# A linear-attention chunk: seven masked products per pair of heads, or one with keys and receptances scaled about the chunk's middle

## The chip, the core and the metric

The kernel runs on one core of a Trainium2 chip. Times are microseconds on the device from the first to the last instruction. A core has five instruction streams that run side by side and wait for each other by semaphores: TensorE (PE: matrix products; its weight loads are shown as PEld), VectorE (DVE), ScalarE (ACT), GpSimd (POOL), and SyncE (SP), which here only starts DMA transfers. An engine with a q behind its name (SPq, ACTq, POOLq) is its sequencer, as when it starts a DMA.

## The reference

Two blocks follow each other. The first is a recurrence over 768 steps for 4 batches of 8 heads with 48 channels:

```python
for t in range(S):
    cur = einsum('bhd,bhe->bhde', u[None] * kt, vt)
    y[:, :, t] = einsum('bhd,bhde->bhe', rt, state + cur)
    state = w[None, :, :, None] * state + einsum('bhd,bhe->bhde', kt, vt)
```

`w`, the decay of each channel, is drawn as `np.random.rand(n_heads, head_dim) * 0.1 + 0.85`, so it lies in 0.85 to 0.95. The 3072 rows of y (4 x 768 tokens, 8 x 48 = 384 columns) go into the second block: gate logits `x @ w_gate` for 8 experts, a greedy balanced assignment (each expert takes exactly 384 tokens, in the order of the logits), and for each expert `relu(x @ w1) @ w2` with a hidden width of 1024. All of it is float32.

## The kernel before

Four stages follow each other on one core.

The **attention stage** (`attention`, L25 to L268) cuts the 768 steps into six chunks of 128. A unit is one chunk of one batch, all 8 heads; there are 24 units, the four batches of a chunk one after the other, so a unit's state comes from four units earlier. Steps stand on the 128 partitions. Two heads are handled together (a pair, four pairs), each padded from 48 to 64 channels.

For a unit, `scale` (L138) loads k, r and v, turns k and r with PE transposes (L146, L151), copies them out of PSUM on ACT (L148, L153), and makes for each of seven levels (64, 32, .., 1 steps) a scaled copy of the keys (POOL, L160) and of the receptances (DVE, two per level for the two heads of a pair, L167; on ACT at the last level, L169). `pairs` (L193) makes for each level four products of 128 x 128 (L200) and lets DVE write those (s, t) that belong to the level into AT, the matrix of pair weights, by a masked copy (L204). `outputs` (L208) multiplies the receptances with the state (L218) and AT with v (L225), adds each step's own term (L228) into x, and brings the state forward (L233, L237, L241). `gate` (L245) turns a unit's x (L251), copies it out on ACT (L253), and multiplies it with the gate's weights (L256) into the logits LG (L258). The written order is `scale(n+1)`, `pairs(n)`, `gate(n-1)`, `outputs(n)`; a scheduler may move instructions of neighbouring units past each other on an engine.

At the end of the stage, x of all tokens and LG lie in SBUF. The **assignment stage** (`assignment`, L271) finds the experts by seven rounds on LG, with small products and DVE operations that wait for each other. Then the rows of x are **scattered** to DRAM in the experts' order (L531), and the **experts stage** (L555 to L576) reads them back and does the two products (L563, L570). The weights of the first two experts are loaded during the attention stage (`before_unit`, L518; L513 and L515): SP starts them as soon as their place in SP's queue is reached.

Of the kernel before, what the change touches and what calls it, by code (L numbers as in the profile page):

```python
# [10 lines left out]
F32 = mybir.dt.float32  # L11
BF16 = mybir.dt.bfloat16
I32 = mybir.dt.int32
U8 = mybir.dt.uint8
AF = mybir.ActivationFunctionType
ALU = mybir.AluOpType
AX = mybir.AxisListType
PSUM = bass.MemoryType.PSUM

NEG = -3.4028234663852886e38  # L20
T = 128
PD = 64


def attention(ctx, tc, r, k, v, w, u, wg, x_all, LG, ident, before_unit):  # L25
    """The recurrence in chunks of 128 steps, and the gate's logits.

    Within a chunk, the pairs (s, t) with s < t are split by halving: at level
    h (64, 32, .., 1) a block of 2h steps has its middle m between s and t, and
    w^(t-1-s) = w^(m-1-s) * w^(t-m), powers from 0 to h-1 only, so that no  # L30
    value of w needs a negative power.
    """
    nc = tc.nc
    B, H, S, D = r.shape
    DX = H * D
    C = S // T
    HP = H // 2
    E = wg.shape[1]
    LEVELS = [64, 32, 16, 8, 4, 2, 1]

    const = ctx.enter_context(tc.tile_pool(name="a_const", bufs=1))
# [26 lines left out]

    # powers of w, with the channels on the partitions: (head of the pair, d)
    wpow = const.tile([128, 8, HP], F32, name="wpow")  # L70
# [29 lines left out]

    # the pairs (s, t) of each level, t over the upper halves
    mask_f = const.tile([128, len(LEVELS), PD], F32, name="mask_f")
# [9 lines left out]

    # The keys of a level count in its lower halves only. The receptances of a
    # pair of heads stand in blocks, so that one product serves both heads.
    ATs, Ks, Rs = [], [], []
# [20 lines left out]
    live = {}  # L136

    def scale(n):  # L138
        """Transposed keys and receptances, and each level's copies of them."""
        load(n + 2)  # L140
# [29 lines left out]

        # a step's own term: r . (u * k) for each head
        rk = pool.tile([128, DX], F32, name="rk")
# [9 lines left out]

        # what reads and writes the state
        rw = kw = None
# [8 lines left out]
    def pairs(n):  # L193
        """The sums over the channels for the pairs of steps of a chunk."""
        kT, K, R, AT = (live[n][x] for x in ("kT", "K", "R", "AT"))
# [12 lines left out]
    def outputs(n):  # L208
        """x, and the state behind the chunk."""
        b, c = units[n]  # L210
# [58 lines left out]


def assignment(ctx, tc, ML, dest, CAP):  # L271
    """Each token's row in the order of the experts.

    The greedy walk down the sorted logits, from one filled expert to the next:
    while no further expert fills, each token goes to its best open one, so the
    next to fill is the one whose CAP-th best token comes first, at the largest
    value that has CAP tokens at or above it for some expert. That value is found
    by its bits, four at a time. Equal logits go by expert and by token.
    """
    nc = tc.nc  # L280
# [32 lines left out]
    for g in range(8):  # L313
        nc.vector.tensor_single_scalar(out=steps[:, g, :], in_=digits, scalar=28 - 4 * g,
                                       op=ALU.logical_shift_left)
    # floats in their order: key = bits ^ (sign ? ~0 : 1 << 31)
    top = const.tile([128, ND], I32, name="top")
# [21 lines left out]
    for _ in range(E - 1):  # L339
        # each token's best open expert  # L340
        m = pool.tile([128, NT], F32, name="m")
# [8 lines left out]

        # the value at which the next expert fills
        cand, bits = top, None
# [28 lines left out]

        # the expert that fills there
        ge = pool.tile([128, NT], F32, name="ge")
# [19 lines left out]

        # its tokens: those above the value, and the first of those at it
        pf = pool.tile([128, NT, E], F32, name="pf")
# [26 lines left out]

        # they and their expert leave
        nc.vector.scalar_tensor_tensor(out=eid, in0=acc, scalar=estar, in1=eid, op0=ALU.mult, op1=ALU.add)
# [5 lines left out]

    # the rest are the last expert's
    rest = pool.tile([128, NT], F32, name="rest")
# [28 lines left out]
def rwkv5_eagle_then_base_layer_balanced(  # L471
# [27 lines left out]
    make_identity(nc, ident)  # L499
    # the rows of x, each with its token's number behind it  # L500
    x_all = keep.tile([128, NT, DX + 1], F32, name="x_all")
# [5 lines left out]
    weights = {}  # L507

    def load_weights(e):
        if e >= E:  # L510
            return
        w1 = wpool.tile([128, KD, F], F32, name="w1")
        nc.sync.dma_start(w1, moe_w1[e].rearrange("(c p) f -> p c f", p=128))  # L513
        w2 = wpool.tile([128, KF, DX], F32, name="w2")
        nc.sync.dma_start(w2, moe_w2[e].rearrange("(c p) d -> p c d", p=128))  # L515
        weights[e] = (w1, w2)

    def before_unit(n):  # L518
        if n in (8, 14):
            load_weights((n - 8) // 6)  # L520

    with ExitStack() as part:
        attention(part, tc, r, k, v, w, u, moe_w_gate, x_all, LG, ident, before_unit)
    with ExitStack() as part:
        assignment(part, tc, LG, dest, CAP)

    # every token has a row of its own, in the experts' order as in out
    xs_rows = dram_disjoint_views(xs_dram, NT)
# [76 lines left out]
```

## Time and profile before

| what | value |
|---|---|
| time, median of 3 runs | 865.85 us (864.2 to 866.3) |
| profiled execution, its span from first to last instruction (the page gives no other time for it) | 865.4 us |
| PE busy | 615.8 us (71%) |
| DVE busy | 457.5 us (53%) |
| POOL busy | 293.0 us (34%) |
| ACT busy | 92.4 us (11%) |

The shares are means over four stages that have little in common. The page cuts the span into 40 slices of 21.6 us; in its lines of busy tenths and of the granted PE clock they stand apart:

```profile
PE   2478899998999988832223322202999999999996
DVE  5968988999989988656665566601001001001000
POOL 7976677686776734000000000073011001001001
PEclk9989999999999999855555555555999999999999
```

A digit is the busy share of a slice in tenths; PEclk is the clock granted to TensorE in tenths of full speed, where 9 or more is its level of 2.4 GHz and 5 its level of 1.2 GHz. The first 17 slices are the attention stage, with PE, DVE and POOL all busy; then comes the assignment with DVE at two thirds and PE at half its clock, then the scatter on POOL, then the experts with PE alone.

### The profile page before, as it was taken

The page shows a single profiled execution, that of the slowest core. Times are in us where ns is not written, and L with a number is a line of the kernel's source. Part 1 is how long each engine was busy: PE and PEld are TensorE (multiplying, and loading weights), DVE is VectorE, ACT ScalarE, POOL GpSimd, SP SyncE. Part 2 cuts the span into 40 slices and gives each one's busy share as a digit, 9 for nine tenths or more (in the row PEclk, how much of TensorE's full clock was granted, in tenths as well). Part 3 has the DMA queues.
Part 4 walks back from the last instruction along what each step waited for, and adds up shares of the span by engine and source line. Part 5 has one row for each costly group of instructions (what it writes and reads, how often), then busy time and mean ns, then how long its engine had stood idle before and what let it go on. Part 6 is the DMA issues. An engine that isn't in the chain of part 4 may idle for free.

```text
span 865.4 us, 11948 instructions
## 1 busy us (share of the span) xinstructions
PE 615.8 (71%) x4723; PEld 486.1 (56%) x4723; DVE 457.5 (53%) x1143; ACT 92.4 (11%) x210; POOL 293.0 (34%) x395
## 2 busy tenths in 40 slices
PE   2478899998999988832223322202999999999996
PEld 1477888888888887722222212101556656656653
DVE  5968988999989988656665566601001001001000
ACT  1011111211112111000000000000110110110110
POOL 7976677686776734000000000073011001001001
PEclk9989999999999999855555555555999999999999
DMA  9252212222122200000000000034334434424100
GB/s 244 94 132 42 47 38 47 47 47 47 37 47 47 47 11 1 1 1 2 1 1 1 1 2 1 1 137 151 114 100 132 170 101 147 163 92 138 45 18 27
DMA packets 93687, 54.48 MB, mean 63 GB/s; under 512 B 76864, under 2 KB 88256, under 8 KB 93632
## 3 DMA queue, kind: packets, MB, share of 16 engines
q1 hardware_dynamic: 86400, 39.33, 16.8%
q0 software_dynamic: 3072, 9.45, 2.9%
q10 hardware_dynamic: 4160, 4.94, 1.7%
q8 instruction: 37, 0.61, 0.3%
q14 instruction: 18, 0.15, 0.1%
HBM read 44.26 MB, written 9.45 MB: 62 GB/s over the span
## 4 chain that ended last, share of the span: by engine, by line
PE 38%; issue 29%; DVE 26%; DMA 2%; POOL 2%; SPq 1%; ACT 0%; POOLq 0%; DVEq 0%; ACTq 0%
DVE AT L204 15%; PE h_ps L563 14%; PE o_ps L570 14%; DVE R L167 8%; PE y_ps L225 6%; PE g_ps L200 2%; DMA w<-in_moe_w_dram 2%; DVE x_all L228 1%; SPq L66 1%; DVE state L241 1%; PE xT_ps L551 1%; POOL K L160 1%; DVE dd L177 1%; DMA xg<-x_sorted 0%; POOL rk L175 0%
## 5 line engine op out<-in xcount | busy, mean ns | idle before, releaser
L200 PE MATMUL g_ps<-R,K 128*128 128x128 f32 x1152 | 152.2, 285 | 4.9 <-DVE AT L204 4.0
L204 DVE COPY_PREDICATED AT<-mask,g_ps 128x512 f32<-128x512 uint8 x168 | 147.8, 882 | 9.3 <-PE g_ps L200 2.3
L200 PEld LDWEIGHTS g_ps<-R,K 128*128 128x128 f32 x1152 | 142.9, 200 | 7.9 <-issue 6.3
L570 PE MATMUL o_ps<-w,hid 128*128 128x384 f32 x384 | 126.2, 486 | 0.0
L563 PE MATMUL h_ps<-xT,w 128*128 128x384 f32 x384 | 125.7, 487 | 0.0
L167 DVE TENSOR_TENSOR R<-rT_ps,pw 64x256 f32<-64x256 f32 x288 | 121.9, 423 | 5.3 <-ACT rT L153 1.5
L160 POOL TENSOR_TENSOR K<-kT,rv 128x256 f32<-128x256 f32 x144 | 94.9, 694 | 84.7 <-ACT kT L148 84.7
L359 PE MATMUL cnt<-prop,ind 128*15 128x8 bf16 x1344 | 42.1, 166 | 97.2 <-DVE ind L337 62.9
L359 PEld LDWEIGHTS <-ind 128*15 128x15 bf16 x1344 | 37.1, 90 | 115.8 <-DVE ind L337 105.9
L563 PEld LDWEIGHTS h_ps<-xT,w 128*128 128x128 f32 x384 | 73.1, 191 | 51.2 <-DVE xT L552 0.4
L570 PEld LDWEIGHTS o_ps<-w,hid 128*128 128x128 f32 x384 | 71.9, 190 | 47.4
L531 POOL DMA_INDIRECT x_sorted<-x_all,dest x24 | 23.3, 970 | 203.7 <-DVE dest L467 196.7
L573 POOL DMA_INDIRECT out_dram<-o_sb,tok x24 | 23.2, 968 | 200.6 <-DVE o_sb L572 175.7
L552 DVE COPY xT<-xT_ps 128x384 f32<-128x384 f32 x24 | 12.7, 555 | 147.8 <-PE xT_ps L551 147.7
L564 ACT ACTIVATE hid<-h_ps 128x384 f32<-128x384 f32 x64 | 31.5, 492 | 445.9 <-PE h_ps L563 445.9
L572 DVE COPY o_sb<-o_ps 128x384 f32<-128x384 f32 x24 | 13.4, 558 | 121.9 <-PE o_ps L570 121.9
L225 PE MATMUL y_ps<-vt,AT 128*128 128x48 f32 x384 | 49.3, 283 | 11.1 <-DVE AT L204 11.0
L225 PEld LDWEIGHTS y_ps<-vt,AT 128*128 128x128 f32 x384 | 46.3, 197 | 15.6 <-DVE AT L204 15.6
L551 PE MATMUL xT_ps<-ident,xg 128*128 128x128 f32 x72 | 11.7, 298 | 40.6 <-DMA xg<-x_sorted 40.5
L151 PE MATMUL rT_ps<-ident,rpad 128*128 128x128 f32 x96 | 23.6, 301 | 16.4 <-ACT R L169 15.7
L551 PEld LDWEIGHTS xT_ps<-ident,xg 128*128 128x128 f32 x72 | 9.6, 154 | 45.5 <-issue 42.2
L361 DVE TENSOR_SCALAR full<-cnt 15x8 bf16<-15x8 f32 x56 | 8.6, 153 | 47.3 <-PE cnt L359 47.3
(133 smaller groups left out, 652.4 us busy)
## 6 DMA issues: line engine op xcount, KB each, us to landing
w<-in_moe_w_dram SPq DMA_DIRECT2D x16, 1536.0 KB, 7.2
xg<-x_sorted ACTq DMA_DIRECT2D x8, 577.5 KB, 6.3
kpad<-in_k_dram SPq DMA_DIRECT2D x24, 192.0 KB, 2.6
rpad<-in_r_dram SPq DMA_DIRECT2D x24, 192.0 KB, 2.6
vt<-in_v_dram SPq DMA_DIRECT2D x24, 192.0 KB, 2.7
x_sorted<-x_all,dest POOLq DMA_INDIRECT x24
out_dram<-o_sb,tok POOLq DMA_INDIRECT x24
u_bc<-in_u_dram ACTq DMA_DIRECT2D x1, 192.0 KB, 4.2
```

The source lines that it names most:

```text
L151: nc.tensor.transpose(rT_ps[:, a, :], pair(rt, a), ident)
L160: nc.gpsimd.tensor_mul(half(K[h], h, 0), half(kT, h, 0), by)
L167: nc.vector.tensor_mul(dst, src, by)
L200: nc.tensor.matmul(g_ps[:, a].rearrange("p q i -> p (q i)"), keys[:, a, :], R[h][:, a].rearrange("p q i -> p (q i)"), start=True, stop=True)
L204: nc.vector.copy_predicated(out=half(AT, h, 1), mask=mk.unsqueeze(1).to_broadcast([128, H, nb, h]), data=g_ps.rearrange("p a q (n i) -> p ...
L225: nc.tensor.matmul(y_ps[:, ds(h * D, D)], AT[:, h, :], vt[:, ds(h * D, D)], start=first, stop=(h == H - 1), skip_group_check=True)
L359: nc.tensor.matmul(cnt, ind[:, i, :], prop[:, i, :], start=(i == 0), stop=(i == NT - 1))
L531: nc.gpsimd.indirect_dma_start(out=xs_rows[i], out_offset=bass.IndirectOffsetOnAxis(ap=dest[:, i:i + 1], axis=0), in_=x_all[:, i, :], in_o ...
L551: nc.tensor.transpose(xT_ps[:, f, :], xg[:, c, ts(f, 128)], ident)
L563: nc.tensor.matmul(h_ps, w1[:, f, ts(j, 128)], xT[:, f, :], start=(f == 0), stop=(f == KD - 1))
L564: nc.scalar.activation(hid[:, j, :], h_ps, AF.Relu)
L570: nc.tensor.matmul(o_ps, hid[:, j, ts(c, 128)], w2[:, j, :], start=(j == 0), stop=(j == KF - 1))
```

## The change

Before the attention stage, DVE tests whether all 384 values of w lie in 0.7 to 1.2. Each engine reads the answer into a register and branches. In that range, `attention_mild` runs; otherwise `attention_any`, which is the old `attention` with nothing in it changed. Both stand in the program.

`attention_mild` writes w^(t-1-s) as w^(t-65) * w^(64-s): the keys of step s are multiplied with w^(64-s), the receptances of step t with w^(t-65). Positive and negative powers both occur (exponents up to 65). These scales are made once (wk, wr, steps on partitions, by powers and reciprocals, L355 and L357), so that a unit scales k and r with one DVE product each before they are turned. One product of 128 x 256 per pair of heads then gives all pairs (s, t) of both heads; DVE multiplies it with a triangle mask into AT. The scaled keys and receptances serve the state as well. Heads are not padded: a pair stands on 96 partitions. ACT writes each head's receptances into a block of its own by a scale of 1 or 0 per partition. The written order runs one step further ahead: `scale(n+2)`, `turn(n+1)`, `pairs(n)`, `outputs(n-1)`, `gate(n-2)`. The core of the diff:

```diff
+def decays_are_mild(ctx, tc, w):
+    nc.sync.dma_start(row, w.rearrange("h d -> (h d)").unsqueeze(0))
+    nc.vector.tensor_single_scalar(out=ge, in_=row, scalar=W_MIN, op=ALU.is_ge)
+    nc.vector.scalar_tensor_tensor(out=both, in0=row, scalar=W_MAX, in1=ge, op0=ALU.is_le, op1=ALU.mult)
+    nc.vector.tensor_reduce(out=flag, in_=both, axis=AX.X, op=ALU.min)
+    return nc.values_load(flag[0:1, 0:1])
...
+    for j in range(7):                      # in attention_mild: powers of w
...
+        nc.vector.tensor_mul(up[:, :, n:n + m], up[:, :, 0:m], by)
+        nc.gpsimd.tensor_mul(down[:, :, L + 1 - n - m:L + 1 - n], down[:, :, L + 1 - m:L + 1], by)
+        nc.vector.tensor_mul(wp[:, j + 1, :], wp[:, j, :], wp[:, j, :])
...
+            nc.vector.reciprocal(ch[:, :, M + 1:T], up[:, :, 1:T - M])
...
+    def scale(n):
...
+        nc.vector.tensor_mul(ks, kt, wk)
+        nc.vector.tensor_mul(rs, rt, wr)
+        nc.gpsimd.tensor_mul(rk, rt, kt)
+        nc.gpsimd.tensor_mul(rk, rk, u_bc)
+        nc.vector.tensor_reduce(out=dd, in_=rk.rearrange("p (h d) -> p h d", h=H), axis=AX.X, op=ALU.add)
+        nc.gpsimd.tensor_mul(yd.rearrange("p (h d) -> p h d", h=H), ...)
+    def turn(n):
...
+        nc.scalar.copy(kT, kT_ps)
+        for q in range(2):
+            nc.scalar.activation(rB[:, :, q, :], rT_ps, AF.Copy, scale=own[:, q:q + 1])
...
+            nc.scalar.copy(rT, rT_ps)
+    def pairs(n):
+        for a in range(HP):
+            nc.tensor.matmul(g_ps[:, 2 * a:2 * a + 2, :].rearrange("p q t -> p (q t)"), kT[:, a, :],
+                             rB[:, a].rearrange("p q t -> p (q t)"), start=True, stop=True)
+        for z in range(2):
+            nc.vector.tensor_mul(AT[:, hs, :], g_ps[:, hs, :], mask.unsqueeze(1).to_broadcast([128, HP, T]))
...
+    for n in range(N + 1):
+        if n + 2 < N:
+            scale(n + 2)
+        if n + 1 < N:
+            turn(n + 1)
+        if n < N:
+            pairs(n)
+        if n > 0:
+            outputs(n - 1)
+        if n > 1:
+            gate(n - 2)
...
     with ExitStack() as part:
-        attention(part, tc, r, k, v, w, u, moe_w_gate, x_all, LG, ident, before_unit)
+        mild = decays_are_mild(part, tc, w)
+    with ExitStack() as part:
+        with tc.If(mild > 0) as which:
+                attention_mild(arm, *arguments)
+        with which.Else():
+                attention_any(arm, *arguments)
```

In `attention_mild` every PSUM tile has one buffer, against two or four for some before. `outputs` and `gate` issue the same products as before (L446, L450, L458, L473, L478), with the state added as a whole on DVE (L462) and multiplied with the chunk's decay on POOL (L463).

On **PE in the steady part of the attention stage**, the rows of one unit before: kT_ps and rT_ps are the turned keys and receptances, g_ps the pair products of a level, y_ps the outputs, kv_ps the new state, xT_ps and lg_ps the gate.

```order
L251 MATMUL xT_ps<-ident,x_all 128x128 x3
L218 MATMUL y_ps<-state_225,rw 128x96 x4
L256 MATMUL lg_ps<-wg_sb,xT 128x8 x3
L233 MATMUL kv_ps<-vt,kw 128x96 x4
L146 MATMUL kT_ps<-ident,kpad_88 128x128 x4
L151 MATMUL rT_ps<-ident,rpad_91 128x128
L200 MATMUL g_ps<-R_1_206,K_1_200 128x128 x4
L200 MATMUL g_ps<-R_1_207,K_1_201 128x128 x4
L151 MATMUL rT_ps<-ident,rpad_91 128x128
L200 MATMUL g_ps<-R_1_208,kT 128x128 x4
L151 MATMUL rT_ps<-ident,rpad_91 128x128 x2
```

The same engine in the same part with the change, one whole unit (ks and rs are the scaled keys and receptances, rB the blocks):

```order
L473 MATMUL xT_ps<-ident,x_all 128x128 x3
L411 MATMUL rT_ps<-ident,rs 96x128 x3
L408 MATMUL kT_ps<-ident,ks 96x128 x2
L478 MATMUL lg_ps<-wg_sb,xT 128x8 x3
L408 MATMUL kT_ps<-ident,ks 96x128 x2
L411 MATMUL rT_ps<-ident,rs 96x128
L428 MATMUL g_ps<-rB,kT 128x256 x4
L446 MATMUL y_ps<-state_190,rT 128x96 x4
L450 MATMUL y_ps<-vt,AT 128x48 x8
L458 MATMUL kv_ps<-vt,ks 96x96 x4
```

Seven groups of four g products became one with twice the columns; between kv_ps of a unit and the next turned keys stand six transposes, three of the gate and three of the receptances. A product of this list stands in the trace as two instructions where its operands are multiplied in float32, and as one where it is a transpose.

On **DVE in the same part** with the change, one unit:

```order
L433 TENSOR_TENSOR AT<-g_ps,mask 128x512 x2
L453 TENSOR_TENSOR x_all<-y_ps,yd 128x384
L388 TENSOR_TENSOR ks<-kt,wk 128x384
L462 TENSOR_TENSOR state_189<-state_189,kv_ps 96x384
L396 TENSOR_REDUCE dd<-rk 128x8
L390 TENSOR_TENSOR rs<-rt,wr 128x384
```

These seven stand for the 23 of a unit before (12 of L167, 7 of L204, 2 of L241, and L228, L177). ks stands behind x_all of the unit whose kv_ps PE is about to make.

At **the start of the program on ACT**, which before begins with its DMAs:

```order
L600 UNCONDITIONAL_BRANCH
L78 DMA u_bc<-in_u_dram 128x384
L79 DMA wg_sb<-in_moe_w_gate_dram 128x3x8
L77 DMA wpow<-in_w_dram 48x4x1 x2
L99 ACT_TABLE_LOAD
L99 COPY wkn<-wk_ps 128x512
```

and with the change reads the flag and branches first:

```order
L845 UNCONDITIONAL_BRANCH
L285 TENSOR_LOAD flag
L763 COMPARE_AND_BRANCH
L328 DMA wp<-in_w_dram 96x4x1
L330 DMA u_bc<-in_u_dram 128x384
L332 DMA wg_sb<-in_moe_w_gate_dram 128x3x8
L363 ACT_TABLE_LOAD
L363 COPY wk<-sc_ps 128x384
L363 COPY wr<-sc_ps 128x384
```

The load of w by channels moved behind the branch, and so did all loads of k, r and v on SP.

## Rows read from the trace of the kernel before

**Rows 1.** Busy time by stretch; columns PE, PEld, DVE, ACT, POOL, clock, DMA share, GB/s.

```profile
0.00:48.74 48.74, 15.27 (x95) 13.92 (x95) 34.93 (x57) 6.86 (x12) 42.09 (x89) 1.00 0.58 158
48.74:360.55 311.81, 282.59 (x2342) 269.71 (x2342) 276.58 (x509) 53.41 (x132) 202.25 (x247) 0.98 0.20 43
...
366.45:602.31 235.86, 57.16 (x1429) 45.68 (x1429) 119.82 (x531) 0.00 (x1) 24.29 (x30) 0.50 0.07 26
...
189.04:202.54 13.50, 12.39 (x105) 11.80 (x105) 12.30 (x24) 2.45 (x6) 9.92 (x13) 1.00 0.23 45
```

**Rows 2.** Chain that ended last, in order of time: start, length, engine and line.

```profile
48.74 3.65 PE y_ps L225 x16
...
360.55 2.02 PE y_ps L225 x16
...
366.45 228.04 issue
...
620.68 15.48 PE o_ps L570 x48
...
855.48 3.96 issue
859.44 1.20 POOLq L600
```

**Rows 3.** Timeline of one unit, weight loads of PE: start, length, line, count.

```profile
202.54 1.86 PEld L225 LDWEIGHTS y_ps<-vt,AT 128*128 128x128 f32 x16 [0.42 <-DVE AT L204]
...
204.32 0.97 PEld L200 LDWEIGHTS g_ps<-R,K 128*128 128x128 f32 x8
...
205.24 0.34 PEld L251 LDWEIGHTS xT_ps<-ident,x_all 128*128 128x128 f32 x3
...
205.54 0.97 PEld L218 LDWEIGHTS y_ps<-state,rw 128*128 128x128 f32 x8
...
206.44 0.75 PEld L256 LDWEIGHTS lg_ps<-wg_sb,xT 128*128 128x128 f32 x6
...
207.97 0.47 PEld L146 LDWEIGHTS kT_ps<-ident,kpad 128*128 128x128 f32 x4
```

**Rows 4.** Groups by line and shape: busy us in all, mean ns of one.

```profile
L204 DVE COPY_PREDICATED AT<-mask,g_ps 128x512 f32<-128x512 uint8 x168 | 147.8, 882 | 9.3 <-PE g_ps L200 2.3
...
L174 POOL TENSOR_TENSOR rk<-rpad,kpad 128x384 f32<-128x384 f32 x24 | 24.1, 1002 | 1.3 <-DVE dd L177 1.3
...
L179 POOL TENSOR_TENSOR yd<-vt,dd 128x384 f32<-128x384 f32 x24 | 20.0, 832 | 1.5 <-DVE x_all L228 0.8 <-DVE dd L177 0.7
...
L153 ACT COPY rT<-rT_ps 128x512 f32<-128x512 f32 x24 | 14.2, 591 | 2.2 <-PE rT_ps L151 2.2
...
L228 DVE TENSOR_TENSOR x_all<-y_ps,yd 128x384 f32<-128x384 f32 x24 | 13.4, 558 | 22.8 <-PE y_ps L225 22.8
```

**Rows 5.** Timeline of the start: start, length, engine, line.

```profile
3.66 1.28 ACT L99 ACT_TABLE_LOAD   x1 [3.66 <-issue]
...
9.61 0.44 DVE L90 TENSOR_TENSOR pw<-pw,wpow 128x256 f32<-128x256 f32 x1
...
12.75 1.12 PE L98 MATMUL wk_ps<-ident,rv 128*128 128x128 f32 x4 [12.75 <-POOL rv L91]
...
15.23 12.73 DVE L111 CAST mask<-mask_f 128x448 uint8<-128x448 f32 x1 [5.07 <-POOL mask_f L107]
```

**Rows 6.** DMA issues of the page: KB each, median us to landing.

```profile
kpad<-in_k_dram SPq DMA_DIRECT2D x24, 192.0 KB, 2.6
...
wpow<-in_w_dram ACTq DMA_DIRECT2D x2, 0.8 KB, 4.8
```

**Rows 7.** A wait of PE and the clock behind it, timeline and stretches.

```profile
345.34 3.66 PE L200 MATMUL g_ps<-R,K 128*128 128x128 f32 x16 [1.48 <-DVE AT L204]
...
346.00:347.00 1.00, 1.00 (x7) 1.00 (x7) 0.81 (x2) 0.00 (x0) 0.00 (x0) 0.50 0.00 0
...
349.00:350.00 1.00, 1.00 (x11) 1.00 (x11) 0.97 (x1) 0.00 (x0) 0.00 (x0) 1.00 0.00 0
```

More of the change, by code (lines that the diff above doesn't have):

```diff
@@ L22, with attention_any @@
 PD = 64
-def attention(ctx, tc, r, k, v, w, u, wg, x_all, LG, ident, before_unit):
+W_MIN, W_MAX = 0.7, 1.2
+def attention_any(ctx, tc, r, k, v, w, u, wg, x_all, LG, ident, before_unit):
     nc = tc.nc
@@ L268, in attention @@
     gate(len(units) - 1)
+def decays_are_mild(ctx, tc, w):
+    nc = tc.nc
+    n = w.shape[0] * w.shape[1]
+    pool = ctx.enter_context(tc.tile_pool(name="mild", bufs=1))
+    row = pool.tile([1, n], F32, name="row")
+    nc.sync.dma_start(row, w.rearrange("h d -> (h d)").unsqueeze(0))
+    ge = pool.tile([1, n], F32, name="ge")
+    nc.vector.tensor_single_scalar(out=ge, in_=row, scalar=W_MIN, op=ALU.is_ge)
+    both = pool.tile([1, n], F32, name="both")
+    nc.vector.scalar_tensor_tensor(out=both, in0=row, scalar=W_MAX, in1=ge, op0=ALU.is_le, op1=ALU.mult)
+    flag = pool.tile([1, 1], I32, name="flag")
+    nc.vector.tensor_reduce(out=flag, in_=both, axis=AX.X, op=ALU.min)
+    return nc.values_load(flag[0:1, 0:1])
@@ L507, in rwkv5_eagle_then_base_layer_balanced, with room_for_weights @@
     weights = {}
+    def room_for_weights(e):
+        w1 = wpool.tile([128, KD, F], F32, name="w1")
+        w2 = wpool.tile([128, KF, DX], F32, name="w2")
+        weights[e] = (w1, w2)
+    for e in range(AHEAD):
+        room_for_weights(e)
     def load_weights(e):
@@ L511, in load_weights @@
             return
-        w1 = wpool.tile([128, KD, F], F32, name="w1")
+        if e not in weights:
+            room_for_weights(e)
+        w1, w2 = weights[e]
         nc.sync.dma_start(w1, moe_w1[e].rearrange("(c p) f -> p c f", p=128))
-        w2 = wpool.tile([128, KF, DX], F32, name="w2")
         nc.sync.dma_start(w2, moe_w2[e].rearrange("(c p) d -> p c d", p=128))
-        weights[e] = (w1, w2)
     def before_unit(n):
@@ L522, in rwkv5_eagle_then_base_layer_balanced @@
     with ExitStack() as part:
-        attention(part, tc, r, k, v, w, u, moe_w_gate, x_all, LG, ident, before_unit)
+        mild = decays_are_mild(part, tc, w)
+    with ExitStack() as part:
+        arguments = (tc, r, k, v, w, u, moe_w_gate, x_all, LG, ident, before_unit)
+        with tc.If(mild > 0) as which:
+            with ExitStack() as arm:
+                attention_mild(arm, *arguments)
+        with which.Else():
+            with ExitStack() as arm:
+                attention_any(arm, *arguments)
     with ExitStack() as part:
```

148 lines of the change are left out of this document (added).

## The prediction

> **What bounds the kernel now.** I read the stretches first, then the chain, then one unit in the timeline, then the groups. The stretches [rows 1] show the attention stage with PE and DVE level: in the unit from 189.04 to 202.54 PE is busy for 12.39 of 13.50 us, DVE for 12.30, POOL for 9.92. Neither waits long, and none alone is full. The chain [rows 2] gives the beats: the first y at 48.74, the last at 360.55. That is 23 periods in 311.8 us, 13.56 each. From the last y the stage needs 5.9 us until DVE can begin the assignment at 366.45. Everything behind (the assignment, 235.9 us up to the first expert product, then the experts with PE alone) computes the same as before with the same instructions, so the change is decided in three places: the time to the first y, the period, and the passage out of the stage.
>
> What a period is made of stands in one unit's weight loads [rows 3], which follow each other nearly without gaps and so show PE's pace: 0.97 us for 8 instructions of a group with 128 columns, 1.86 for the 16 of y, 0.47 for four transposes, 0.34 for the gate's three, 0.75 for its six products. Seven levels of 0.97 are 6.8; with the state product (0.97), y (1.86), kv (as the state product, 0.97), both turns (2 x 0.47), the gate (0.34 + 0.75) a unit needs 12.6 us of PE. The real period is 7% longer. So PE's list nearly fills the period, and DVE's list nearly does too.
>
> **The period after.** On PE six of the seven levels go, and the seventh has 256 columns. The trace has no product of 256; the second expert product has 384 columns and goes at 15.48 / 48 = 0.322 us [rows 2], so per column 0.84 ns, and 256 cost 0.215. Bounds: not under 0.121 (a 128-column product, above), not over 0.322. Eight of them are 1.72 us (1.0 to 2.6). The rest of the list stays: 0.94 turns, 0.97 state, 1.86 y, 0.97 kv, 1.09 gate. Sum 7.55 us, and 6.58 in the four units of the first chunk, which read no state.
>
> The other engines go under this. DVE: AT takes two instructions of 512 elements from PSUM; the masked copy of 512, waits for the shared ports and PSUM included, took 0.88 us on average, the sum of x of 384 took 0.56 [rows 4]. With 2 x 0.88 and five of about 0.56 (x, ks, state, dd, rs, all of 384 elements) DVE needs 4.6 us. POOL: two products of rk (1.0), yd and the state's decay (0.83 each) [rows 4], 3.7 us; its six key copies of a unit (L160) and two scaled operands of the state (L187, L190) are gone. ACT: four copies of 512 at 0.59, the gate's two under 0.6: 3.0 us. So PE becomes the one bound of the stage, and DVE, POOL and ACT, half idle, hide what the change adds on them.
>
> Does the order let PE run through? Two hand-overs in each unit are short. After kv, DVE must make ks (0.56 and two hand-overs of about 0.1) before PE can turn the keys that stand three units ahead, as ks has three buffers; in between PE has three gate transposes and three of the receptances, 0.34 + 0.35 us. That leaves about 0.1 uncovered. After the gate's transposes, ACT copies (0.5 and two hand-overs) before the gate's products; five transposes, 0.6, stand between: again about 0.1. The single PSUM buffers do not bite: g_ps is read by DVE within 2 us and written again some 6 us later. I take the 7% that the stage has over PE's list today: 8.1 us a period, 7.0 in the first chunk. Bounds are 7.55 (no wait) and, with each hand-over wholly open, below under the rivals. 3 x 7.0 + 20 x 8.1 = 183 us. PE begins cold: its first transposes took 1.12 us for four against 0.47 [rows 5, 3] and its first y 3.65 against 2.02 [rows 2], 1.6 us lost there; I allow 2. Together 185 against 311.8: **126.8 us less.**
>
> A sentence of the Trainium skill would put this lower: "TensorE: Matmul & The Clock Gate", part 2, says that a weight load takes time by its columns, and the turns and kv now load 96 columns instead of 128. By it 16 of a unit's instructions of about 0.12 us would be a quarter shorter, as an estimate 0.5 us a unit, and the time 11 us lower. No load of 96 columns is in this trace, all float32 ones have 128, so I leave it as part of the low end.
>
> **The start.** Today's first y at 48.74 stands behind POOL and DVE: the conversion of the level masks on DVE from 15.23 took 12.7 us [rows 5], and the stage's fills keep POOL busy for 42 of 48.7 us [rows 1]. Both belong to the old arm now. In their place: SP issues w's row at 0.8; landing 2.6 as a load of k [rows 6]; three DVE instructions on 384 elements, 3 x 0.56: 5.1. Then each engine reads the flag, branches and joins the others: no row shows it; it cannot be below nothing, and the end of the program, where all engines meet and finish, took 3.96 + 1.20 = 5.2 [rows 2]; I take the middle, 2.6: 7.7. w by channels must now be loaded behind it, 4.8 [rows 6]: 12.5. Seven steps of powers at up to 0.44 [rows 5], 3.0: 15.5. Reciprocals of 260 elements: at least 0.44, at most the 12.7 of the slowest DVE instruction of the trace; 1.0, near the ordinary ones: 16.5. Scales for the keys: four cold transposes 1.12, ACT's table load 1.28 [rows 5], copy 0.59; for the receptances 1.12 + 0.59: 21.2. rs 0.56, transposes 1.12, two block copies 1.18: 24.1. Cold g: 8 x 0.43: 27.5. AT 1.6: first y at **29.1**, 19.6 us earlier. Its bounds are 25 and 45.
>
> **The passage out.** The tail of 5.9 stays (its products are the same). All engines then jump over the old arm and DVE waits for all of them: between nothing and 5.2, I take **2.6** again. For the jump only a page has a rule: the Trainium skill, "Runtime: NRT & Kernel Launch", section "Instruction fetch mechanics", says that a taken branch to a place not yet fetched stalls until it is loaded. No taken jump stands inside this trace, so it stays within those ends.
>
> DMA: 24 units bring the same bytes in a shorter stage, 43 GB/s at 20% share [rows 1] become about 72 at a third; loads run three units, 24 us, ahead. The first experts' weights now start later in SP's queue, behind half the units' loads, so they no longer sit in the start.
>
> **Sum**, against the profiled execution (865.4, 0.45 under the median of the runs, which I leave in the rounding): 865.4 - 126.8 - 19.6 + 2.6 = 721.6, **722 us**.
>
> **Rivals.** (1) PE waits in every unit. For it: every PSUM tile has one buffer, PE takes its list in order, and the two hand-overs above have no slack; DVE takes its list in order too, so a late dd (which waits for POOL) pushes rs, AT and ks. Against: DVE is half idle. A wait of 1.48 us at 343.86 was followed by half clock [rows 7]: the 16 instructions behind it took 3.66 us against 1.94 at full clock, and at 349 the clock was full again. If that came in each unit, 1.5 + 1.7 us more, 23 x 3.2 = 74: **796 us**. With waits of half a microsecond and no fall of the clock it is 734, which is still the forecast's case.
>
> (2) DVE's ks and rs collide with POOL. The trace's products of two operands from SBUF beside a busy POOL took 0.44 us for 256 elements [rows 5], no more than their size asks; it has few. If each ks waits for a POOL instruction of 1.0 us [rows 4] and ks stands in the hand-over of kv, PE loses up to 1.0 a unit: **745 us**. The Trainium skill, "SBUF — State Buffer", "Who interferes with whom", says that a DVE instruction with two SBUF inputs and a GpSimd one that reads SBUF exclude each other for a whole instruction; that speaks for it, the row above does not.
>
> (3) Slower: PE stays at its lower clock, 1.2 GHz, through the stage, as it does through the assignment (0.50 at 57 us of PE in 236) [rows 1]. Its place is the period: each instruction doubles, 15.1 us plus 0.5 of hand-overs, 15.6: 722 + 20 x 7.5 + 3 x 6.6 = **892 us**. It decides from a period of 14.3, where the 20 + 127 us are used up. Against: PE would be busy for nearly all of that period, and after the wait in rows 7, with PE busy, the clock was full again at 349.
>
> (4) The change does not do what it says: the old arm runs. Then the test and both joins come on top: 865 + 7.7 + 2.6 = **876 us**. w lies in 0.85 to 0.95, inside the test's limits, so this needs a mistake in reading the flag.
>
> **From these the numbers.** The forecast, PE bound with a period of 7.5 to 8.6, has 0.64, by itself 708 to 737; rival 2 has 0.12; rival 1, whole or in part (745 to 800), 0.20; rival 3 0.02; rival 4 0.02. Eight in ten lie from 700 (period 7.4, start at 25) to 775 (half of rival 1, or rival 2 with a start of 45 and a join of 5). Faster by over 0.3%, which is about what a measurement of this kernel can tell from no change, 0.95; within it 0.01; slower 0.04.
>
> **What would show it.** The beat of y in the chain: 8.1 us. PE's busy share in the steady part over 90%, DVE's under 60%, the granted clock at 1.0 (rival 1: 0.5 in part of each unit, with an idle of PE ended by DVE or ACT before the turned keys or the gate). First y near 29 and not past 40; from the last LG to the first assignment instruction under 5 us. ks at 0.56 us and not 1.5 (rival 2). The assignment and the experts as long as before. The forecast is wrong if the period is over 9.5 or the first y is past 45.

## The result

The changed kernel takes 694.82 us (median; 692.04 to 695.86) against 866.08 us: a ratio of 0.802, with an interval of 0.800 to 0.804. The forecast of 722 had the direction and the place right, and its time was 27 us too long; the measured time lies 5 us under the range. The profiled execution has a span of 694.1 us, against 865.4 before.

### The profile page after: what moved, and what is told of

The parts are those of the page before. It is cut to its first block, busy times and chain, and to the rows that moved or that the text cites. A ratio compares the mean times of both kernels' runs of the same rounds, so it can differ in the third digit from the quotient of the medians.

```text
span 694.1 us, 8915 instructions
## 1 busy us (share of the span) xinstructions
PE 485.4 (70%) x3575; PEld 358.0 (52%) x3575; DVE 262.9 (38%) x763; ACT 100.7 (15%) x207; POOL 142.7 (21%) x170
## 4 chain that ended last, share of the span: by engine, by line
PE 66%; DVE 21%; issue 5%; POOL 4%; DMA 1%; ACT 0%; SPq 0%; POOLq 0%; ACTq 0%; DVEq 0%
PE h_ps L808 18%; PE o_ps L815 17%; PE cnt L588 6%; PE g_ps L428 6%; PE y_ps L450 6%; DVE ind L566 4%; POOL x_sorted L776 3%; PE y_ps L446 2%; PE lg_ps L478 2%; DVE ks L388 2%; PE kv_ps L458 2%; PE kT_ps L408 2%; DVE dg L594 1%; PE dg_ps L592 1%; DVE bits L604 1%
## 5 line engine op out<-in xcount | busy, mean ns | idle before, releaser
L797 DVE COPY xT<-xT_ps 128x384 f32<-128x384 f32 x24 | 12.7, 554 | 147.8 <-PE xT_ps L796 147.6
L428 PE MATMUL g_ps<-rB,kT 96*128 96x256 f32 x192 | 47.4, 386 | 0.0
L450 PE MATMUL y_ps<-vt,AT 128*128 128x48 f32 x384 | 46.2, 273 | 0.0
L450 PEld LDWEIGHTS y_ps<-vt,AT 128*128 128x128 f32 x384 | 45.5, 193 | 0.4 <-DVE AT L433 0.2
L433 DVE TENSOR_TENSOR AT<-g_ps,mask 128x512 f32<-128x512 f32 x48 | 30.9, 685 | 24.4 <-PE g_ps L428 24.2
L428 PEld LDWEIGHTS g_ps<-rB,kT 96*128 96x128 f32 x192 | 35.0, 194 | 3.8
L398 POOL TENSOR_TENSOR yd<-vt,dd 128x384 f32<-128x384 f32 x24 | 21.5, 894 | 54.3 <-DVE x_all L453 52.4
L416 ACT ACTIVATE rB<-rT_ps,own 96x512 f32<-96x512 f32 x48 | 30.7, 682 | 4.7 <-PE rT_ps L411 4.6
L393 POOL TENSOR_TENSOR rk<-rt,kt 128x384 f32<-128x384 f32 x24 | 26.8, 1117 | 4.8 <-DMA kt<-in_k_dram 3.2
```

What stands on the lines that cost most here:

```text
L393: nc.gpsimd.tensor_mul(rk, rt, kt)
L416: nc.scalar.activation(rB[:, :, q, :], rT_ps, AF.Copy, scale=own[:, q:q + 1])
L428: nc.tensor.matmul(g_ps[:, 2 * a:2 * a + 2, :].rearrange("p q t -> p (q t)"), kT[:, a, :], rB[:, a].rearrange("p q t -> p (q t)"), start=T ...
L433: nc.vector.tensor_mul(AT[:, hs, :], g_ps[:, hs, :], mask.unsqueeze(1).to_broadcast([128, HP, T]))
L450: nc.tensor.matmul(y_ps[:, ds(h * D, D)], AT[:, h, :], vt[:, ds(h * D, D)], start=first, stop=(h == H - 1), skip_group_check=True)
```

## Time and profile after

The stretches of the changed kernel, cut where [rows 1] cuts those of before: up to the first y, from the first to the last y, the tail up to DVE's first instruction of the assignment, the assignment with the scatter, and one unit.

```profile
0.00:25.70 25.70, 11.45 (x54) 9.64 (x54) 16.75 (x35) 6.07 (x10) 17.14 (x35) 1.00 0.67 131
25.70:186.43 160.73, 153.45 (x1226) 143.83 (x1225) 100.37 (x151) 61.95 (x130) 76.96 (x76) 1.00 0.47 109
186.43:194.34 7.91, 6.51 (x36) 5.61 (x34) 0.56 (x2) 1.24 (x4) 0.00 (x0) 0.59 0.02 4
194.34:432.26 237.92, 58.83 (x1436) 46.78 (x1436) 120.80 (x532) 0.05 (x1) 24.31 (x30) 0.50 0.07 26
95.64:103.31 7.67, 7.07 (x59) 6.61 (x58) 4.83 (x9) 2.86 (x6) 5.45 (x6) 1.00 0.76 242
```

The first y comes 23.0 us earlier (25.70 against 48.74), the 23 periods are 151.1 us shorter (160.73 against 311.81), the tail is 2.1 us longer (7.91 against the 5.85 from the last y at 360.55 to DVE's `ones` at 366.40), and everything behind `ones` is 0.8 us longer (499.8 against 499.0). PE is now busy for 95% of the stage and DVE for 62%, so PE is the bound.

One unit on PE, in its timeline (start, length, line, count, and in brackets idle time and what ended it):

```profile
95.64 1.91 PE L450 MATMUL y_ps<-vt,AT 128*128 128x48 f32 x16
97.39 0.88 PE L458 MATMUL kv_ps<-vt,ks 128*96 128x96 f32 x8
98.11 0.49 PE L473 MATMUL xT_ps<-ident,x_all 128*128 128x128 f32 x3
98.44 0.49 PE L411 MATMUL rT_ps<-ident,rs 128*96 128x128 f32 x3
99.52 0.42 PE L408 MATMUL kT_ps<-ident,ks 128*96 128x128 f32 x2 [0.60 <-DVE ks L388]
99.78 0.73 PE L478 MATMUL lg_ps<-wg_sb,xT 128*128 128x8 f32 x6
100.37 0.40 PE L408 MATMUL kT_ps<-ident,ks 128*96 128x128 f32 x2
100.61 0.27 PE L411 MATMUL rT_ps<-ident,rs 128*96 128x128 f32 x1
100.72 1.89 PE L428 MATMUL g_ps<-rB,kT 96*128 96x256 f32 x8
102.45 0.25 PE L446 MATMUL y_ps<-state,rT 96*128 96x96 f32 x1
```

Read the starts, not the lengths: a group's length holds the end of its last product, which runs beside the next group's first. From start to start y takes 1.75 (not 1.91), kv 0.72, the gate's transposes 0.33, its products 0.59, the g products 1.73. The state's eight run from 102.45 to the next y at 103.31, 0.86. With the two turns (0.33 + 0.26 + 0.24 + 0.11 = 0.94) PE's list is 6.92 us. The rest of the 7.67 is the gap before the turned keys, 0.75, of which the row names 0.60 as a wait for ks.

The timeline of DVE and POOL there shows why ks is late, and one unit further a ks that isn't:

```profile
97.59 0.56 DVE L453 TENSOR_TENSOR x_all<-y_ps,yd 128x384 f32<-128x384 f32 x1 [1.32 <-PE y_ps L450]
98.22 0.83 POOL L398 TENSOR_TENSOR yd<-vt,dd 128x384 f32<-128x384 f32 x1 [1.43 <-DVE x_all L453]
98.31 1.16 DVE L388 TENSOR_TENSOR ks<-kt,wk 128x384 f32<-128x384 f32 x1 [0.16 <-PE kv_ps L458]
...
105.98 0.56 DVE L388 TENSOR_TENSOR ks<-kt,wk 128x384 f32<-128x384 f32 x1 [0.16 <-PE kv_ps L458]
```

`yd` has three buffers. x_all frees one, POOL starts the next `yd` at once, and 0.09 us later DVE starts ks. Beside it ks takes 1.16 us; at 105.98 POOL is idle and it takes 0.56. Over the kernel ks and rs cost DVE 1.02 and 0.92 us on average, against the 0.56 of the sum of x [rows 4], in the groups by shape (busy us in all, mean ns):

```profile
L388 DVE TENSOR_TENSOR ks<-kt,wk 128x384 f32<-128x384 f32 x24 | 24.4, 1024 | 2.8 <-PE kv_ps L458 2.4 <-PE kT_ps L408 0.4
L390 DVE TENSOR_TENSOR rs<-rt,wr 128x384 f32<-128x384 f32 x24 | 22.1, 922 | 6.2 <-PE rT_ps L411 6.2
```

The start in the timeline, from the test to the first g products:

```profile
2.19 0.35 DVE L280 TENSOR_SCALAR ge<-row 1x384 f32<-1x384 f32 x1 [2.19 <-DMA row<-in_w_dram]
4.36 0.41 SPq L321 DMA_DIRECT2D kt<-in_k_dram  x1
7.46 0.19 DVE L346 TENSOR_TENSOR up<-up,wp 96x4 f32<-96x4 f32 x1 [1.35 <-DMA wp<-in_w_dram]
9.25 1.72 DVE L355 RECIPROCAL wk_ch<-up 96x252 f32<-96x252 f32 x1
11.49 1.76 DVE L357 RECIPROCAL wr_ch<-down 96x260 f32<-96x260 f32 x1
22.03 2.89 PE L428 MATMUL g_ps<-rB,kT 96*128 96x256 f32 x8
```

The flag is ready at 3.69 (its reduction starts at 3.15 and takes 0.54); reading it, branching and joining take 0.67 us until SP issues the first load of k (4.36). The longest wait is for w's channels, 4.57 to 7.44. PE still runs at its low clock here: the eight g products at 22.03 take 2.89 us, those of the steady unit above 1.89.

The tail and the way out on PE and DVE:

```profile
186.43 2.21 PE L450 MATMUL y_ps<-vt,AT 128*128 128x48 f32 x16
189.93 1.45 PE L478 MATMUL lg_ps<-wg_sb,xT 128*128 128x8 f32 x6 [0.62 <-ACT xT L475]
192.74 1.45 PE L478 MATMUL lg_ps<-wg_sb,xT 128*128 128x8 f32 x6 [0.62 <-ACT xT L475]
194.34 0.17 DVE L518 MEMSET ones<- 128x128 bf16 x1 [5.03 <-PE lg_ps L478]
...
199.70 0.62 PE L588 MATMUL cnt<-prop,ind 128*15 128x8 bf16 x19 [1.03 <-issue]
```

Two gates instead of one stand in the tail, most of it at 1.2 GHz (0.59 is the stretch's mean). What the clock makes of this tail is shown under the version without a branch and with the powers on DVE. DVE does not wait at the join: `ones` starts with the end of the last gate's copy. PE stops once, for 1.03 us, five products into the assignment, and waits for nothing that the trace shows.

## Experiments

Each is one change of the changed kernel (694.82 us), unless it says otherwise; ratios are to the kernel before.

**More buffers for yd, for ks, and for both.**

```diff
-        yd = pool.tile([128, DX], F32, name="yd", bufs=3)
+        yd = pool.tile([128, DX], F32, name="yd", bufs=5)      # yd5
-        ks = pool.tile([128, DX], F32, name="ks", bufs=3)
+        ks = pool.tile([128, DX], F32, name="ks", bufs=4)      # ks4; ks4yd5 has both
```

> yd has five buffers instead of three, so that POOL's product yd no longer waits for x_all and no longer starts just ahead of DVE's ks. If ks is slow because it and POOL's yd shut each other out: ks back at 0.55 us in most units (1.16 in the steady part of the changed kernel), the wait of PE for the turned keys (6.9 us in all) nearly gone, steady period 7.5 to about 7.1, and the time 694.8 to about 689. If ks is slow for a reason of its own (its operands, its shape): ks stays at 1.16 and the time at 695. If POOL's rk or the state's decay takes yd's place beside ks: ks between the two, 690 to 695.

> ks has four buffers instead of three, so that ks of the unit three ahead no longer waits for this unit's kv_ps and PE's turned keys do not stand behind that hand-over; POOL and DVE may shut each other out as before. If the hand-over kv_ps, ks, kT_ps is what the steady period has above PE's own list (6.9 us between starts): period 6.9 to 7.2, time about 688. If PE's list itself takes 7.5: 695, no change.

> Both buffers. If each of them opens the same wait: as ks4 alone, 687 to 689. If POOL and DVE shutting each other out also holds up others (AT, rs): 1 to 3 us below ks4. If neither matters: 695.

Measured: yd5 689.62 us (ratio 0.7961, 0.7943 to 0.7979), ks4 691.72 (0.7993, 0.7977 to 0.8010), ks4yd5 690.84 (0.7985, 0.7966 to 0.8005). The stretch of the 23 periods and the group of ks with five buffers for yd:

```profile
24.20:178.60 154.40, 152.90 (x1225) 143.66 (x1225) 91.44 (x151) 61.59 (x130) 77.83 (x78) 1.00 0.49 114
...
L388 DVE TENSOR_TENSOR ks<-kt,wk 128x384 f32<-128x384 f32 x24 | 17.5, 736 | 3.0 <-PE kv_ps L458 2.3 <-PE kT_ps L408 0.8
```

The same instructions with the same PE busy time, but `yd` no longer starts when x_all does: ks falls to 736 ns on average, PE is busy for 99% of the stretch, and the commonest periods are 6.89 us, PE's bare list (eight times), and 7.21 (seven times). So the late ks cost 6.3 us of the 23 periods (154.40 against 160.73). The 5.2 by which the time fell is not this alone: in the profiled execution of yd5 the first y also came 1.5 us earlier, and the tail and what follows took 1.9 longer. The start is the same program in both; PE's clock was up sooner in this execution, as its first g products show (2.89 us above):

```profile
21.52 1.89 PE L428 MATMUL g_ps<-rB,kT 96*128 96x256 f32 x8
```

With four buffers for ks every steady period is 7.21, where 6.9 to 7.2 was expected: PE no longer waits for ks, which now comes before the turned receptances in its list, but the weight loads of the gate's products wait for ACT's copy of xT, 0.33 in each of 17 units (5.6 us in all). One short hand-over took the place of the other, and both buffers together bring no more than ks4: the 23 periods take 157.21 in either, 3.5 less than in the changed kernel. Of the three intervals only that of yd5 lies apart from the changed kernel's (0.800 to 0.804), so what ks4 brings is read from the stretch.

**The g products twice.**

```diff
             nc.tensor.matmul(g_ps[:, 2 * a:2 * a + 2, :].rearrange("p q t -> p (q t)"), kT[:, a, :], ...)
+            nc.tensor.matmul(g_ps[:, 2 * a:2 * a + 2, :].rearrange("p q t -> p (q t)"), kT[:, a, :], ...)
```

> Each pair product is issued twice (the same result), 8 more PE instructions of 256 columns a unit, 1.72 us. If PE's list bounds the period: 24 x 1.72 = 41 us more, less the 5 to 7 us of waits that it may cover: 730 to 736. If a chain through DVE or ACT bounds it and PE has slack: under half of that, 700 to 715.

Measured: 736.45 us (0.8506, 0.8480 to 0.8533), 41.6 more. The steady period is 9.40: the old 7.67 and 1.73. The eight new products stand in full on the path, beside the old wait of 0.75 for ks; PE's list is the bound, and 1.73 is what it counts for them.

**AT multiplied twice.**

```diff
             nc.vector.tensor_mul(AT[:, hs, :], g_ps[:, hs, :], mask...)
+            nc.vector.tensor_mul(AT[:, hs, :], g_ps[:, hs, :], mask...)
```

> DVE makes each half of AT twice (the same result), 1.37 us more of DVE in a unit: 5.9 of a period of 7.7. If PE's list bounds the period and DVE hides: 695 to 705, the few us from the longer way from g_ps to AT and from a list in another order. If DVE, or the way g_ps, AT, y_ps, sets the period: 24 x 1.37 = 33 us more, 728.

Measured: 716.21 us (0.8266, 0.8237 to 0.8294), 21.4 more, which neither theory gave. In the steady part AT takes DVE 2.73 us a unit instead of 1.37, and the period is 7.67, the commonest one without it, so DVE's additional time is hidden there. (PE's list stands in another order, with its waits in other places, so the equal period is in part chance.) The loss is in the end: two stretches in the last units.

```profile
180.57:191.72 11.15, 9.78 (x44) 8.70 (x42) 3.94 (x7) 0.64 (x2) 0.00 (x0) 0.58 0.01 3
191.72:204.02 12.30, 10.95 (x43) 9.67 (x42) 3.09 (x5) 0.64 (x2) 0.00 (x0) 0.50 0.00 0
```

The scheduler put the second half of a unit's y behind the next unit's g and before its state product. Without kv and turns between them PE waits 0.62 for the gate and 0.74 for x_all in each of the last three units; the clock falls to 0.50 and stays there. The changed kernel has one such wait for x_all in its last units, 0.47 ahead of the last y. That the waits bring the clock down is read from what follows what, and was not tried. From the first y of the third last unit to DVE's `ones` it takes 33.7 us (180.57 to 214.22), in the changed kernel 17.6 (176.71 to 194.34): 16 of the 21 us. Another 3.9 were lost up to there, and 1.3 behind it.

**No branch.**

```diff
-        mild = decays_are_mild(part, tc, w)
-        with tc.If(mild > 0) as which: ...
+        attention_mild(part, *arguments)
```

> The new attention runs without the test of w, the flag and the branch; the old arm is not in the program. If the branch costs only its time at the start (first load of k issued at 4.36 us instead of 0.82) and what one engine waits behind the jump (1.03 us of PE ahead of its sixth counting product): 3.5 to 4.6 us less, about 690.5. If the branch also parts the schedules (instructions can't move over its borders) or the jump costs several us on DVE: 686 or less. As predicted before the result (2.6 for flag and branch, 1.7 for the test, 0.8 to 4.8 behind it, 2.6 for the way out): 6.9 to 10 less.

Measured: 697.49 us (0.8047, 0.8023 to 0.8070): not faster, against the expectation. The loads start 3.5 us sooner (SP's first k at 0.81), but the first y is at 25.53. Two rows of POOL's timeline, and DVE's second reciprocal:

```profile
7.06 1.00 POOL L393 TENSOR_TENSOR rk<-rt,kt 128x384 f32<-128x384 f32 x1 [0.49 <-DMA rt<-in_r_dram]
...
11.09 0.51 POOL L347 TENSOR_TENSOR down<-down,wp 96x128 f32<-96x128 f32 x1
...
11.64 1.78 DVE L357 RECIPROCAL wr_ch<-down 96x260 f32<-96x260 f32 x1 [0.29 <-POOL down L347]
```

The receptances come before the powers are done, POOL puts its products rk between them, and the reciprocal that needs the last power starts at 11.64, where it started at 11.49. The 23 periods take 1.1 longer (161.83). In the end the clock falls inside the last unit's y (3.54 us for its 16 products against 2.21), and the tail takes 9.24, 1.3 more. In the other direction, PE's stop of 1.03 in the assignment is gone (its 24 cnt products follow each other).

**No branch, with the powers of POOL on DVE** (compared with no_branch).

```diff
-        nc.gpsimd.tensor_mul(down[:, :, L + 1 - n - m:L + 1 - n], down[:, :, L + 1 - m:L + 1], by)
+        nc.vector.tensor_mul(down[:, :, L + 1 - n - m:L + 1 - n], down[:, :, L + 1 - m:L + 1], by)
```

> No branch, and the seven growing products of the negative powers on DVE instead of POOL. The version without a branch (697.5 us) had its loads 3.5 us earlier but its first y at 25.53, since POOL made its products rk between the powers and so ended them at 11.6. Theory (POOL's order ate the gain of the early loads): reciprocals of the receptances' scale begin at about 7.5 to 8.5 instead of 11.64, first y at 22 to 23.5, time 694 to 695.5, so that a branch costs some 3 us. Rival (something else holds the start, as the loads or the transfer of r): first y at 25 or later and 697 to 698.

Measured: 695.80 us (0.8048, 0.8025 to 0.8071), with the first y at 25.54. The theory of POOL's order among the powers is not borne out. The powers now wait on DVE, and the reciprocal begins at 11.31 again:

```profile
7.11 0.93 DVE L348 TENSOR_TENSOR wp<-wp 96x4 f32<-96x4 f32 x1
7.97 3.15 DVE L347 TENSOR_TENSOR down<-down,wp 96x4 f32<-96x4 f32 x7
11.31 1.77 DVE L357 RECIPROCAL wr_ch<-down 96x260 f32<-96x260 f32 x1
```

The seven products follow the first reciprocal, as DVE takes its list in order, and stretch to 3.15 us beside POOL's rk; a four-element product at 7.11 took 0.93, and the same shape 0.15 elsewhere. But it is not what the first y waits for. Two rows from DVE's and PE's timelines:

```profile
23.55 0.55 DVE L396 TENSOR_REDUCE dd<-rk 128x8 f32<-128x384 f32 x1 [2.28 <-POOL rk L394]
25.54 1.09 PE L450 MATMUL y_ps<-vt,AT 128*128 128x48 f32 x8 [1.25 <-DVE AT L433]
```

The g products ahead of the first y start at 21.52, 1.3 us earlier than in no_branch; then AT stands behind dd and rs in DVE's list, and dd waits 2.28 for POOL's rk. So the rival holds in its first part: something else, POOL's products rk, keeps the first y at 25.5.

The profiled executions of these two versions lie 3.8 us apart, and 3.5 of it is the tail, which ran here at the full clock:

```profile
187.43 1.91 PE L450 MATMUL y_ps<-vt,AT 128*128 128x48 f32 x16
...
193.14 0.17 DVE L518 MEMSET ones<- 128x128 bf16 x1 [3.13 <-PE lg_ps L478]
```

From the last y to `ones` it takes 5.71 us here and in g_twice, 7.91 in the changed kernel, and 9.24 in no_branch, whose clock was at 1.2 GHz throughout. The instructions are the same.

**The loads of w by channels, u and the gate's weights ahead of the test,** alone and with yd5.

```diff
+        early = early_loads(part, tc, w, u, moe_w_gate)   # wp, u_bc, wg_sb on ACT's queue
         mild = decays_are_mild(test, tc, w)
```

> The loads of w by channels, of u and of the gate's weights start before the test instead of behind the branch; all else as in the changed kernel (694.8 us). Theory (the wait for w's channels, which land at 7.44, is what the branch costs at the start: powers begin at 7.46 and everything up to the first y hangs on them): w's channels have landed by 3.9, powers begin right behind the join at about 4.7, the first y comes 2.7 us earlier, at 23.0, and the time is 692 us (691 to 693). Rival (the first y hangs on POOL, which has to do the powers, the products rk and yd in turn, and on the loads of r, which still start behind the branch): first y within 1 us of 25.7, time 694 to 696.

> Five buffers for yd and the early loads together. If both gains are independent (5.2 us from the collision of ks with yd, 2.7 us from the start), 687 us (685.5 to 688.5), the fastest version so far (five buffers alone 689.6). If the first y hangs on POOL: 689 to 691.

Measured: wp_early 692.56 us (0.8004, 0.7984 to 0.8024), yd5_wp 691.85 (0.7999, 0.7971 to 0.8027). The first y of the first:

```profile
22.08 1.09 PE L462 MATMUL y_ps<-vt,AT 128*128 128x48 f32 x8 [0.74 <-DVE AT L445]
```

The powers begin at 4.79, right behind the join, and the transposes of the first scales at 9.30, 1.9 us earlier. The first y comes 3.6 us earlier than in the changed kernel, but 2.1 earlier than in yd5, which has the changed kernel's start and had its clock up sooner; so some 2 us are the early loads' and the rest the clock's. The time is lower by 2.3, which the intervals do not tell apart from none: the last y ran at the low clock (3.54 us), and the tail gave 1.3 back (9.24). With yd5 the gains do not add: the stage ends at 187.71, with yd5 alone at 187.14. The first y is 2.2 us earlier than there (22.01), but the 23 periods take 2.1 longer (156.53) and the tail 0.6. Most of the 2.1 is one period of 8.53, in which dd came late (DVE waits 1.96 for POOL's rk) and ks with it, and PE waited 1.46. yd5 remains the lowest median, though the four times of yd5_wp are 689.4 twice and 694.3 twice.

**The other arm** (limit 0.9, so that w is out of range).

```diff
-W_MIN, W_MAX = 0.7, 1.2
+W_MIN, W_MAX = 0.7, 0.9
```

> The upper limit of w is 0.9, so that the test fails for these inputs and the old arm runs. If entering costs what it costs the new arm (3.5 us at the start) and leaving nothing: 866 + 3.5 to 5 = 870 to 871. If reaching the far arm, behind the new arm's code, stalls for each engine as well: 873 to 878; the prediction gave 876.

Measured: 866.75 us (1.0009, 0.9996 to 1.0021), no difference. SP's first load is at 4.76 instead of 0.82 and the first y at 53.45, 4.7 us later, yet DVE's `ones` is at 365.55, 0.9 earlier. The kernel before began its products cold just behind that point; here the low clock lies ahead of it. This is the stretch from 40 to 60 us in this arm:

```profile
40.00:50.00 10.00, 6.70 (x30) 6.30 (x31) 6.97 (x13) 1.32 (x3) 8.89 (x9) 0.50 0.57 144
50.00:60.00 10.00, 9.08 (x77) 8.42 (x77) 7.30 (x15) 2.24 (x6) 6.38 (x9) 1.00 0.78 271
```

and in the kernel before:

```profile
40.00:50.00 10.00, 5.64 (x46) 5.45 (x45) 6.87 (x11) 1.17 (x2) 9.48 (x12) 0.92 0.21 42
50.00:60.00 10.00, 9.74 (x64) 9.42 (x64) 7.32 (x17) 1.28 (x4) 7.38 (x8) 0.74 0.66 183
```

The first period takes 13.55 us instead of 18.96. That the shift of the clock paid for the test is read from these rows and was not tried by itself. On the way out this arm's 24 cnt products run without a stop.

**The written order of before with the new arithmetic** (`scale(n+1)`, `turn(n+1)`, `pairs(n)`, `gate(n-1)`, `outputs(n)`; the diff is shortened).

```diff
-    for n in range(N + 1): scale(n+2); turn(n+1); pairs(n); outputs(n-1); gate(n-2)
+    for n in range(N): scale(n+1); turn(n+1); pairs(n); gate(n-1); outputs(n)
```

> The new arithmetic in the written order of before: scale and turn of the next unit, pairs, gate of the last unit, outputs of the same unit, so that y_ps of a unit follows its own AT. If the gain comes from PE's shorter list, and PE finds the next unit's turns to do meanwhile: 695 to 710. If the deeper order is what keeps PE from waiting for AT (g_ps, 1.4 us of DVE, two hand-overs, in each unit): 24 x 1.5 = 36 us more, 730, with falls of the clock up to 760.

Measured: 700.33 us (0.8079, 0.8053 to 0.8104). So 165.8 of the 171.3 us come without the deeper order, which brings 5.5. Counted from one state product to the next, eight of the sixteen full periods are 6.93 to 6.95 us, PE without a gap; four are over 10, each behind a wait for AT of 1.5 to 1.75, as this one in PE's timeline, with the clock of the stretches behind it:

```profile
88.60 1.09 PE L450 MATMUL y_ps<-vt,AT 128*128 128x48 f32 x8 [1.50 <-DVE AT L433]
```

```profile
88.60:92.00 3.40, 3.40 (x27) 3.36 (x28) 1.58 (x4) 0.00 (x0) 0.40 (x1) 0.83 0.00 0
92.00:95.58 3.58, 3.58 (x17) 3.10 (x16) 2.98 (x4) 2.31 (x4) 3.58 (x4) 0.68 0.96 191
```

AT is late since DVE's list has dd ahead of it and dd waits for POOL's rk. This is rival 1 in small: wait and half clock together made the period from 85.23 to 95.58 10.35 us, 3.4 over the others.

## Why the prediction was right or wrong

The sum of the prediction's steps against the trace, in us:

| step | predicted | measured | too long by |
|---|---|---|---|
| first y | 29.1 | 25.70 | 3.4 |
| 23 periods | 185 | 160.73 | 24.3 |
| tail | 5.9 | 7.91 | -2.0 |
| passage out | 2.6 | 0 at the join, 0.8 behind it | 1.8 |

**The period: the mechanism was right, its size was not, and this is the step that failed.** PE became the one bound, DVE fell to 62% (under 60 was forecast), the clock stayed at 1.0. The term of the 23 periods, 185, measured 160.7, for two reasons. First, "PE's list" was summed from the lengths of weight-load groups in [rows 3], and these overlap. The rows themselves say so: y at 202.54 has 1.86 and the g group behind it starts at 204.32, 1.78 later; that has 0.97 and the transposes start at 205.24, 0.92 later. By starts, the list is 6.92 and not 7.55: y 0.11 less, the state's products 0.11, the gate 0.17, kv 0.25; the turns (0.94) and the 256-column products (1.73 against 1.72) are as forecast, and the doubled g products show their 1.73 as time. For the same reason the "7%" was no measure of PE's waits before, as it was taken over a list that was too long. The wait of PE after is 0.57 a period (7.49 less 6.92, the mean of 16 periods from 50.42 to 170.20), near the 0.55 that the margin gave: right by accident.

Second, the sum took every period behind the first chunk as full. The last chunk has no kv and no state to bring forward, the last units have nothing left to turn, and the first ones no gate. By place, the 24.3 split into 9.8 of these 16 periods (0.61 each), 6.4 in the first four (24.7 against 3 x 7.0 + 8.1 + the 2 for a cold PE) and 8.1 in the last three (16.2 against 24.3). By reason, the same sum with 7.49 for 8.1 (and 6.63 in the first chunk) gives 171.7: 13.3 of the 24.3 are the list, and 11.0 the periods that are not full.

DVE's 4.6 us a unit, against 4.72 measured, was right by luck: AT took 0.69 an instruction and not 0.88, ks and rs 1.02 and 0.92 and not 0.56.

kv is not quite the product of before: it loads 96 columns where it loaded 128. For it the sentence from the Trainium skill ("TensorE: Matmul & The Clock Gate", part 2, weight loads by columns) is borne out: inside a group its products start 0.085 us apart, those of the state, with 128 columns loaded and the same 96 moved, 0.112. For the turns it is not: they load 96 columns as well and start 0.109 apart, as they did before with 128. That is about 0.2 a unit, not the 0.5 estimated there.

**Rival 2 was real, at about a quarter of its price** (6.3 us of the 23 periods, where 23 were set). ks takes 1.16 instead of 0.56 when POOL's yd starts just ahead of it. The prediction set row L90 of [rows 5] against this; when that one instruction started, POOL had 0.16 us left of a product of two operands (from 9.54, 0.23 long), too little to show in it, and so the row was no evidence. The rule named there (the Trainium skill, "SBUF — State Buffer", "Who interferes with whom") agrees with this trace in the main: 1.16 is the 0.74 that yd still has when ks starts, and 0.42 for the product itself, which takes 0.56 alone. PE loses 0.75 in such a unit, not 1.0, since six transposes cover part of it, and not every unit has it. PE's two "uncovered 0.1" hand-overs were the right places: the first is this one, the second is what ks4 turned it into.

**Rival 1 and 3** did not come in the changed kernel: the clock is 1.00 from the first to the last y. old_order and at_twice show PE's waits followed by the low clock, where PE's order leaves gaps. **Rival 4** did not come; the arm itself costs no measurable time (0.9996 to 1.0021), where 876 was forecast.

**The start** was 3.4 too long, with errors of both signs. The row and the test ended at 3.7 (5.1), the branch and join took 0.67 (2.6), w's channels 2.9 (4.8); the powers 1.8 (3.0). The reciprocals were 3.5 together where 1.0 was taken: the bounds of 0.44 to 12.7 held it, and the choice "near the ordinary ones" was wrong. So both scales were there at 15.4 (21.2). From there to the first y it took 10.3 and not 7.9, since PE makes turns and kv of further units ahead of the first g, at its low clock. wp_early shows that the chain up to the scales bears on the first y, with some 2 us; no_branch and no_branch_dve show that it isn't alone, and that a removed test moves other work into its place. No run parts the 23.0 us by which the first y moved into the masks and the fills.

**The tail** was called unchanged. One more unit's gate stands behind the last y, but that alone costs nothing: at the full clock the same tail takes 5.71 (no_branch_dve). The 2.0 are the low clock's. **The passage out** cost nothing at the join. A stop of PE of 0.6 to 1.4 some 5 us behind `ones` is there in every version whose new arm jumps but g_twice (1.03 in the changed kernel), and not in no_branch, no_branch_dve or else_arm. The stretch from `ones` to the first expert product is 237.9, without a branch 236.5 and 236.3, but 237.2 in g_twice and 237.5 in the kernel before, which has no branch either; so that the stop lengthens it is not shown. That the stop is the jump to a place not yet fetched (the rule of "Runtime: NRT & Kernel Launch", "Instruction fetch mechanics", in the Trainium skill) fits, but no run tells it from another cause.

## What to carry to other kernels

Sum an engine's list from start to start, never from the lengths of groups, and count what each of the first and last units really has. Where DVE multiplies two operands from SBUF, look at which instruction on POOL starts at the same event; a buffer more for POOL's result can move it out of the way. Before a difference of 2 or 3 us is put down to a change, compare the stretches that the change cannot touch: the same start and the same tail came out 1.5 and up to 3.5 us apart with the clock. Before the removal of a wait is given a price, write down the next thing in that engine's list, since a scheduler moves work into the gap.

## What the runs showed of the hardware

- A DVE product of 384 elements with both operands in SBUF took 0.56 us beside an idle POOL and 1.16 us beside a POOL product that started 0.09 us earlier; POOL's own products (rk) took 1.0 alone and up to 1.35 beside DVE.
- RECIPROCAL of 252 and 260 elements took 1.72 and 1.76 us on DVE, 6.8 ns an element, against 1.5 for an ordinary product of 384 (0.56 us).
- At the full clock, instructions of a float32 product inside a group start 0.112 us apart with 128 columns loaded, whether 48 or 96 are moved (y, the state's); 0.085 with 96 loaded and 96 moved (kv); 0.216 with 256 moved (g). Transposes start 0.109 apart with 96 or 128 loaded and 128 moved.
- The same tail, from the last y to the assignment, took 5.71 us at the full clock (a mean of 0.98, no_branch_dve) and 9.24 at 1.2 GHz (0.50, no_branch).
- A flag read by all engines, with branch and join, took 0.67 us from the end of its last instruction to the first DMA behind it.
